# Two attention-fed mixes in one program: the first two sequence tiles joined in the second mix, softmax work moved, three weight sums put on TensorE

## The chip, the cores and the metric

One core of one Trainium2 chip. The metric is device time in microseconds of one execution, median over runs. TensorE (PE) multiplies, VectorE (DVE), ScalarE (ACT) and GpSimd (POOL) do the elementwise work, and SyncE (SP) issues every DMA.

## The reference

Three stages follow each other over 2 batches of 4160 tokens of width 192. The first is a causal seven-tap weighted sum whose weights are a softmax. The second ("first mix") mixes each token with its predecessor, multiplies by `w_k` (192 x 1024), squares the relu, multiplies by `w_v`, and gates with a sigmoid. The third ("second mix") multiplies by `w_in`, takes relu, convolves three taps over the tokens, gates, and multiplies by `w_out`.

```
w = softmax(weight_gen, axis=taps)                       # 8 heads x 7 taps
x = sum_k w[k] * x_padded[token + k]                     # (2, 4160, 192)
xk, xr = mu * x + (1 - mu) * x_prev                      # one pair of mu each
y = sigmoid(xr @ w_r) * (maximum(xk @ w_k, 0) ** 2 @ w_v)
h = maximum(y @ w_in, 0)
c = conv_w[0] * h[t-1] + conv_w[1] * h[t] + conv_w[2] * h[t+1]
out = (h * sigmoid(c)) @ w_out
```

The weights arrive as float64. A product keeps float32 accuracy by splitting each operand into a rounded part and its rest, so that each product is five matmul passes.

## The kernel before, in words

The sequence is cut into ten tiles (`SIZES`): 256, 248, seven of 472, and 352 tokens. All of the program is first written as a list of closures with due times (`at(t, fn)`, tile i around `T = 16*i`). `Program.schedule` then walks this list with its own table of costs (`cost`), and puts out the instructions in the order in which its clock would start them. Each engine gets its instructions in that fixed order: an instruction that waits holds up all that stand behind it on its engine. Every instruction is recorded by the one line in `schedule`, so views go by tile names, not lines.

- `softmax(j, ...)` works on block j of the weights `sw`: block 0 for tile 0, 1 for tile 1, 2 for tile 2, 3 for tiles 3 to 9. Its steps are a maximum (DVE), a subtraction (POOL; DVE for block 0), an Exp (ACT), a sum (DVE), a reciprocal (DVE) and a multiplication (POOL; DVE for block 0).
- `attention(i, b, ...)` makes tile i of batch b in "tokens" of 128 rows: four POOL operations each (`prod`, twice `prod<-prod`, `tok`). Tiles 0 and 1 have two such tokens in each batch, the 472-wide tiles four.
- `mixing(i, u, ...)` transposes `tok` on TensorE (`flip`: `pa<-ident,tok`), mixes neighbours, splits into rounded part and rest (the rest on POOL from tile 1 on: `xA<-mk,xA`, `mk<-mk,rm`). u=0 takes 128 columns of batch 0, u=1 of batch 1, u=2 the 64 left of each, so it needs all tokens of both. What u=2 makes goes by DMA to `xB`, without which no product of either batch is finished.
- `moe1(i, b, fi)` is one of eight blocks of the first mix: five passes into one of two banks `pa`, three ACT steps and one DVE step there (`s`), five passes into `am` and `ar`. `gate_r` makes the sigmoid gate, `mix_out` applies it and writes the tile into `x2[b]`.
- `moe2(i, b, fi)` is a block of the second mix: five passes into one of two banks `pc`, four ACT and four DVE steps (`h`, `pc`, `g`), five passes into `bm` and `br`. It runs `LAG` = 10 after `moe1`.
- `prepare` makes float32 weights of the float64 ones, 16 chunks: `narrow` builds the value of a chunk from its two halves with one ACT and five DVE operations, `split` writes rounded part and rest. The chunks of `w_k`, `w_v`, `w_r` come first, those of `w_in` and `w_out` after.

```
for i in range(NTILE):
    T = 16 * i
    ...
            for u, t in ((0, T - 5), (2, T - 3.7), (1, T + 3)) if i > 1 else ((0, 7), (2, 8.3), (1, 15)):
                mixing(i, u, t, 2.5)
    for b in range(NB):
        t = T + 8 * b
    ...
        for fi in range(NF):
            moe1(i, b, fi, t + fi)
            moe2(i, b, fi, t + fi + LAG)
        mix_out(i, b, t + 8.52)
        store(i, b, t + LAG + 10.02)
```

Of the kernel before, what the change touches and what calls it, by code (L numbers as in the profile page):

```python
# [26 lines left out]
LAG = 10  # L27
# [8 lines left out]
class Program:  # L36
# [37 lines left out]
    def cost(self, eng, method, out, ins, pointer):  # L74
# [12 lines left out]
        if eng == "DVE":  # L87
            if method == "tensor_reduce":
                n = self.count(ins[0])
# [6 lines left out]
        if eng == "POOL":  # L96
            busy = 0.1 + (n / 455 if method == "tensor_tensor" else n / 270)
            return busy, busy + 0.12
        return 0.6, 0.6

    def schedule(self):
# [4 lines left out]
        for i, (eng, method, a, k, _, hold) in enumerate(self.ops):  # L106
# [3 lines left out]
            ins = [x for x in aps if x is not out]  # L110
# [33 lines left out]
        for _ in range(n):  # L144
# [17 lines left out]
            for j in succ[i]:  # L162
                ready[j] = max(ready[j], t + dur[i] if eng == "PE" == self.ops[j][0] else end)
                left[j] -= 1
                if not left[j]:
                    open_[self.ops[j][0]].append(j)
# [17 lines left out]
def conv_moe_kernel(ctx: ExitStack, tc: tile.TileContext, xp, wg_first, wg_rest, mus, w_k, w_v, w_r, w_in, conv_w, w_out, out):  # L184
# [42 lines left out]
    ident = new("ident", [128, 128])  # L227
    wkA = new("wkA", [128, 2, DFF], F32R)
# [14 lines left out]
    wb_r = Ring([early[:, :1024].rearrange("p (a b) -> p a b", a=2)])  # L243
    rows_r = ring("rows", 2, [128, max(SLOTS) + PAD, DM])
# [9 lines left out]
    g_r = ring("g", 2, [128, 2, W], F32R)  # L254
# [54 lines left out]

    def narrow(st, n):  # L310
# [5 lines left out]
        ACT.activation(px, f(hi), ACTF.Copy, scale=2.0 ** -112)  # L316
        DVE.tensor_scalar(x, x, 3, None, op0=ALU.logical_shift_left)
# [57 lines left out]
    def prepare(first, seq):  # L375

        for j, (t, (load, n, go)) in enumerate(seq):
# [5 lines left out]
            def use(st=st, n=n, go=go):  # L383
                go(narrow(st[0], n))
# [10 lines left out]
    def softmax(j, a, b, eng, times, bank):  # L395
# [58 lines left out]
    def mixing(i, u, t, dt_):  # L454
        N, P, e = SIZES[i], PART[i], EXTRA[i]
        c = 1 if u == 2 else 0
        st = {}

        def flip():
            p = pa_r()  # L460
            st["p"] = p[:, e:e + N]
            st["q"] = p
            x = tok_t[i]
            k = (0, 256, 128)[u]
            for l in range(SLOTS[i]):
# [15 lines left out]
        def m1(k):  # L481
            st[k] = (am_r, ar_r)[k]() if i == 0 else mk_r()
            col = 2 * k + c
            own = slice(col, col + 1)
            if i < 2:
                a = shifted(lambda y, x: ACT.activation(y, x, ACTF.Copy, scale=onemu[:, own]))
                DVE.scalar_tensor_tensor(out=st[k][:, :N], in0=st["p"], scalar=mu[:, own], in1=a, op0=ALU.mult, op1=ALU.add)
            else:
                DVE.scalar_tensor_tensor(out=st[k][:, :N], in0=st["d"], scalar=onemu[:, own],
                                         in1=st["p"], op0=ALU.mult, op1=ALU.add)  # L490

        def hi(k):
# [6 lines left out]
            ACT.copy(x[:, 0, :N], st[k][:, :N])  # L499

        def lo(k):
            x = st["h", k]
            y = x[:, 1, :N] if u < 2 else (mk_r() if i == 0 else st[k])[:, :N].bitcast(F32R)
            (POOL if i else DVE).tensor_tensor(y, st[k][:, :N], f(x[:, 0, :N]), op=ALU.subtract)
            if u == 2:
                for b in range(NB):
# [5 lines left out]
                    SP.dma_start(out=f(z[oth, :N]), in_=f(y[own]))  # L512
# [98 lines left out]
    def mix_out(i, b, t):  # L611
        N = SIZES[i]
        X = x2[b]
        c = slice(2, N + 2)
# [11 lines left out]
        def a1():  # L626
            ACT.copy(X[:, 2, c], r[:, :N])
            ACT.copy(X[0:64, 3, c], r[0:64, :N])
# [18 lines left out]
    def moe2(i, b, fi, t):  # L647
        last = i == NTILE - 1
        N = SIZES[i] + (2 if last else 0)
# [201 lines left out]
```

## Time and profile before

| | |
|---|---|
| median of 3 runs | 779.31 us (778.96 to 781.27) |
| profiled execution | 780.29 us, of which its span 778.5 us |
| busy PE, ACT, DVE, POOL | 694.1, 665.5, 630.8, 506.6 us |
| mean granted clock of TensorE | 0.974 |
| idle time of PE by its largest releaser | 35.6 us, 4 times, POOL's `tok` |

All times in the profile count from the start of the span. Busy time is a sum over stages that differ much: the first 160 us, in which weights are prepared and two small tiles run, and the rest. So they are read by stretches and by single places in the program. In a row of a timeline, "x3" means three instructions merged, and the brackets at its end hold how long the engine was idle and what ended it.

### The profile page before, as it was taken

The page shows a single profiled execution, that of the slowest core. Times are in us where ns is not written, and L with a number is a line of the kernel's source. Part 1 is how long each engine was busy: PE and PEld are TensorE (multiplying, and loading weights), DVE is VectorE, ACT ScalarE, POOL GpSimd, SP SyncE. Part 2 cuts the span into 40 slices and gives each one's busy share as a digit, 9 for nine tenths or more (in the row PEclk, how much of TensorE's full clock was granted, in tenths as well). Part 3 has the DMA queues.
Part 4 walks back from the last instruction along what each step waited for, and adds up shares of the span by engine and source line. Part 5 has one row for each costly group of instructions (what it writes and reads, how often), then busy time and mean ns, then how long its engine had stood idle before and what let it go on. Part 6 is the DMA issues. An engine that isn't in the chain of part 4 may idle for free.

```text
span 778.5 us, 10782 instructions
## 1 busy us (share of the span) xinstructions
PE 694.1 (89%) x3505; PEld 606.3 (78%) x3505; DVE 630.8 (81%) x1137; ACT 665.5 (85%) x1441; POOL 506.6 (65%) x368
## 2 busy tenths in 40 slices
PE   0065776999999999999999999999999999999985
PEld 0054676898888888888888888888888888888974
DVE  6997977886878787878787888788788878788886
ACT  2466797998989898989998989898989899999985
POOL 6998888899999999999999798565702010110000
PEclk9996886999999999999999999999999999999999
DMA  7685010130130112111221120120002000200000
GB/s 224 197 269 180 4 52 11 58 105 11 62 101 18 53 70 51 70 51 52 69 70 51 39 78 20 45 63 7 20 0 70 1 19 1 57 0 19 19 2 28
DMA packets 19240, 45.09 MB, mean 58 GB/s; under 512 B 3056, under 2 KB 14704, under 8 KB 19056
## 3 DMA queue, kind: packets, MB, share of 16 engines
q1 hardware_dynamic: 19184, 44.41, 18.9%
q8 instruction: 27, 0.44, 0.2%
q14 instruction: 29, 0.24, 0.1%
HBM read 27.40 MB, written 6.39 MB: 43 GB/s over the span
## 4 chain that ended last, share of the span: by engine, by line
PE 68%; ACT 14%; DVE 14%; issue 2%; DMA 1%; SPq 0%; ACTq 0%; DVEq 0%
PE pa L169 21%; PE pc L169 16%; PE am L169 10%; PE bm L169 9%; PE ar L169 7%; PE br L169 6%; DVE pc L169 4%; ACT pa L169 2%; DVE stage L169 2%; ACT pc L169 2%; ACT h L169 2%; ACT g L169 2%; ACT L169 1%; DVE bm L169 1%; DVE s L169 1%
## 5 line engine op out<-in xcount | busy, mean ns | idle before, releaser
L169 DVE SCALAR_TENSOR_TENSOR pc<-h,cw,pc 128x472 f32<-128x472 f32 (+3 forms) x312 | 203.7, 653 | 34.9 <-ACT pc L169 31.9
L169 POOL TENSOR_TENSOR prod<-rows,sw 128x1344 f32<-128x1344 f32 x70 | 216.1, 3087 | 11.0 <-DMA rows<-in_x_dram 6.0
L169 ACT ACTIVATE pa<-pa 128x472 f32<-128x472 f32 (+3 forms) x324 | 162.7, 504 | 37.9 <-PE pa L169 33.8
L169 POOL TENSOR_TENSOR prod<-prod 128x576 f32<-128x576 f32 (+1 forms) x140 | 171.2, 1223 | 8.6
L169 PE MATMUL am<-s,wv 128*128 128x472 f32 (+3 forms) x480 | 146.9, 366 | 7.5 <-ACT s L169 6.0
L169 PE MATMUL bm<-g,wo 128*128 128x472 f32 (+3 forms) x465 | 144.5, 361 | 9.6 <-ACT g L169 9.0
L169 DVE TENSOR_TENSOR pc<-h,pc 128x472 f32<-128x472 f32 (+3 forms) x156 | 92.6, 594 | 54.4 <-ACT pc L169 53.0
L169 PE MATMUL pa<-xA,wkA 128*128 128x472 f32 (+3 forms) x480 | 124.4, 363 | 7.5 <-DVE s L169 3.5
L169 PE MATMUL pc<-x,wiA 128*128 128x474 f32 (+3 forms) x468 | 118.6, 361 | 3.2 <-DVE g L169 3.2
L169 POOL TENSOR_TENSOR xA<-mk,xA 128x472 fp32r<-128x472 f32 (+2 forms) x36 | 40.5, 1130 | 122.1 <-ACT xA L169 95.8
L169 PE MATMUL ar<-s,wv 128*128 128x472 f32 (+3 forms) x320 | 112.0, 362 | 5.0 <-DVE x L169 3.3
L169 PE MATMUL br<-g,wo 128*128 128x472 f32 (+3 forms) x310 | 109.4, 356 | 0.0
L169 DVE TENSOR_TENSOR s<-pa,s 128x472 fp32r<-128x472 f32 (+3 forms) x162 | 94.9, 586 | 16.0 <-ACT s L169 15.0
L169 PEld LDWEIGHTS am<-s,wv 128*128 128x128 f32 x480 | 88.7, 196 | 22.4 <-ACT s L169 11.2
L169 DVE TENSOR_TENSOR g<-pc,g 128x472 fp32r<-128x472 f32 (+3 forms) x153 | 90.4, 591 | 16.4 <-ACT g L169 14.9
L169 PEld LDWEIGHTS bm<-g,wo 128*128 128x128 f32 x465 | 86.5, 192 | 21.1 <-ACT g L169 11.5
L169 PEld LDWEIGHTS pa<-xA,wkA 128*128 128x128 f32 x480 | 86.4, 196 | 19.8 <-DVE s L169 6.3
L169 ACT ACTIVATE pc<-h,cw 128x472 f32<-128x472 f32 (+3 forms) x156 | 97.5, 625 | 1.6
L169 PEld LDWEIGHTS pc<-x,wiA 128*128 128x128 f32 x468 | 84.3, 194 | 14.0 <-DVE g L169 4.5
L169 ACT ACTIVATE h<-pc 128x474 f32<-128x474 f32 (+3 forms) x156 | 82.5, 529 | 9.6 <-PE pc L169 7.5
L169 PE MATMUL pa<-xB,wkB 128*128 128x472 f32 (+3 forms) x320 | 89.0, 359 | 1.1 <-DMA xB<-mk 1.1
L169 PE MATMUL pc<-x,wiB 128*128 128x474 f32 (+3 forms) x312 | 87.4, 359 | 0.0
(121 smaller groups left out, 1086.9 us busy)
## 6 DMA issues: line engine op xcount, KB each, us to landing
rows<-in_x_dram SPq DMA_DIRECT2D x14, 960.0 KB, 4.5
xB<-rm SPq DMA_DIRECT2D x28, 118.0 KB, 2.3
xB<-mk SPq DMA_DIRECT2D x28, 118.0 KB, 2.3
out_dram<-om SPq DMA_DIRECT2D x14, 236.0 KB, 2.0
rows<-in_x_dram SPq DMA_DIRECT2D x4, 768.0 KB, 6.6
rows<-in_x_dram SPq DMA_DIRECT2D x2, 864.0 KB, 4.3
out_dram<-ob SPq DMA_DIRECT2D x14, 118.0 KB, 2.2
stage<-in_moe_w_v_dram SPq DMA_DIRECT2D x4, 384.0 KB, 3.8
```

The source lines that it names most:

```text
L169: getattr(self.real[eng], method)(*a, **k)
```

## The change

- The second tile shrinks from 248 to 220 tokens, the seven wide ones grow from 472 to 476.
- In the second mix, tiles 0 and 1 become one unit of 476 (`UNIT`, `OFFSET`): tile 0 writes its part of `x2[b]`, and no `moe2` and no `store` run for it; `moe2` and `store` of tile 1 work on 476 tokens.
- `narrow` and `split` of the first three weight chunks (`on_pe`): the sum of the halves is a float32 matmul with the identity and one with the rounded identity, the rounded part is subtracted by a matmul with its negative, and ACT copies the rest out. Three DVE additions and four DVE subtractions go (two of the four are of one chunk). A tile `signs` holds the two matrices.
- The chunks of `w_in` and `w_out` are due later; blocks 1 and 3 of the softmax are due at other times; of block 3, tile 3 keeps its own Exp, and those of tiles 4 to 9 are done by one Exp over 46 columns of slots.
- The scheduler's costs of POOL, `tensor_reduce` and float32 matmuls change; a flip transposes its last token first; tile 0's mix keeps its values in one bank `ar`.
- Two more kinds of `mixing` (u = 3, 4) are written and not called.

```
-SIZES = [256, 248] + [472] * 7 + [352]
+SIZES = [256, 220] + [476] * 7 + [352]
+OFFSET = [0, SIZES[0]] + [0] * (NTILE - 2)
+UNIT = [None, SIZES[0] + SIZES[1]] + SIZES[2:]
...
+            if method == "matmul" and ins[0].dtype == F32:
+                n *= 4
...
-                n = self.count(ins[0])
+                return 0.05 + self.count(ins[0]) / 515, 0.15 + self.count(ins[0]) / 515
...
-            busy = 0.1 + (n / 455 if method == "tensor_tensor" else n / 270)
-            return busy, busy + 0.12
+            busy = 0.15 + (n / 455 if method == "tensor_tensor" else n / 270)
+            return busy, busy + 0.1
...
+        if on_pe[0]:
+            zr = wz_r()[:, :n]
+            DVE.tensor_scalar(x, x, 3, None, op0=ALU.logical_shift_left)
+            DVE.scalar_tensor_tensor(out=z, in0=hi, scalar=0x80000000, in1=x, op0=ALU.bitwise_and, op1=ALU.bitwise_or)
+            DVE.tensor_scalar(y, z, 0xFF800000, None, op0=ALU.bitwise_and)
+            DVE.scalar_tensor_tensor(out=zr, in0=lo, scalar=2.0 ** -52, in1=py, op0=ALU.mult, op1=ALU.mult)
+            PE.matmul(px, lhsT=ident, rhs=f(z), start=True, stop=False, skip_group_check=True)
+            PE.matmul(px, lhsT=signs[:, 0:128], rhs=zr, start=False, stop=True, skip_group_check=True)
+            return px
...
-        DVE.tensor_tensor(dst_lo, x, f(dst_hi), op=ALU.subtract)
+        if on_pe[0] and prog.space(x) == "PSUM":
+            PE.matmul(x, lhsT=signs[:, 128:256], rhs=dst_hi, start=False, stop=True, skip_group_check=True)
+            ACT.copy(dst_lo, x)
+        else:
+            DVE.tensor_tensor(dst_lo, x, f(dst_hi), op=ALU.subtract)
...
-        c = slice(2, N + 2)
+        c = slice(OFFSET[i] + 2, OFFSET[i] + N + 2)
...
-        N = SIZES[i] + (2 if last else 0)
+        N = UNIT[i] + (2 if last else 0)
...
-    softmax(1, 0, slots[1], POOL, (-82.6, -82.5, -82.4, -82.35, -82.3, -82.25), ar_r.tiles[0])
+    softmax(1, 0, slots[1], POOL, (-83.85, -83.65, -83.64, -83.63, -83.62, -83.55), am_r.tiles[0])
...
-        softmax(3, a, b, POOL, (16.5 + 0.3 * j, 16.6 + 0.3 * j, 19.5 + 0.1 * j, 20.5 + 0.5 * j, 20.6 + 0.5 * j, 24.9 + 16 * j), None)
+        softmax(3, a, b, POOL, (30.3, 30.4, 31.2, 32.0, 32.1, 34.9) if j == 0 else
+                (36.9 + 1.2 * j, 37 + 1.2 * j, None, 30 + 16 * j, 30.1 + 16 * j, 32.5 + 16 * j), None)
+    a = slots[3]
+    at(45.3, lambda: ACT.activation(sm[3][0][:, a:], sm[3][0][:, a:], ACTF.Exp))
...
-                moe2(i, b, fi, t + fi + LAG)
+                if i:
+                    moe2(i, b, fi, t + fi + LAG)
             mix_out(i, b, t + 8.52)
-            store(i, b, t + LAG + 10.02)
+            if i:
+                store(i, b, t + LAG + 10.02)
```

What the change does to the order shows at three places. The first is the beginning on DVE: block 0 of the softmax (`sw`, `am`, `smz`) ends with the multiplication of `sw` that the first token on POOL needs, and the first weight chunk begins with a shift in bank `bm`. Before:

```order
L169 TENSOR_REDUCE am<-sw 128x32
L169 TENSOR_SCALAR am<-am 128x32
L169 RECIPROCAL smz_108<-am 128x32
L169 TENSOR_TENSOR sw<-sw,smz_108 128x224
L169 TENSOR_SCALAR bm<-bm 128x512
```

And of the change:

```order
L175 TENSOR_REDUCE am<-sw 128x32
L175 TENSOR_SCALAR bm<-bm 128x512
L175 TENSOR_SCALAR am<-am 128x32
L175 SCALAR_TENSOR_TENSOR stage<-stage,bm 128x512
L175 RECIPROCAL smz_109<-am 128x32
L175 TENSOR_SCALAR pc_114<-stage 128x512
L175 TENSOR_TENSOR sw<-sw,smz_109 128x224
```

The shift (`bm<-bm`), which waits for a weight from memory, stood behind the multiplication of `sw`; now it and two more operations of the chunk stand ahead of it.

The second place is on POOL behind the fourth token of tile 2 before, and behind the eighth of it in the change; `sw<-sw,stage` are operations of block 3 of the softmax, `prod` and `tok` those of a token. Before:

```order
L169 TENSOR_TENSOR prod<-prod 128x384
L169 TENSOR_TENSOR sw<-sw,stage 128x448 x2
L169 TENSOR_TENSOR tok_79<-prod 128x192
L169 TENSOR_TENSOR sw<-sw,stage 128x448 x4
L169 TENSOR_TENSOR sw<-sw,stage 128x336
L169 TENSOR_TENSOR prod<-rows_76,sw 128x1344
L169 TENSOR_TENSOR sw<-sw,stage 128x448
```

And of the change:

```order
L175 TENSOR_TENSOR prod<-prod 128x576
L175 TENSOR_TENSOR prod<-prod 128x384
L175 TENSOR_TENSOR tok_82<-prod 128x192
L175 TENSOR_TENSOR xA_90<-mk_86,xA_90 128x476
L175 TENSOR_TENSOR xA_92<-mk_87,xA_92 128x476
L175 TENSOR_TENSOR sw<-sw,stage 128x448 x2
L175 TENSOR_TENSOR mk_86<-mk_86,rm_88 128x476
L175 TENSOR_TENSOR sw<-sw,stage 128x448 x2
L175 TENSOR_TENSOR mk_87<-mk_87,rm_89 128x476
L175 TENSOR_TENSOR sw<-sw,stage 128x448
```

Seven subtractions of block 3 stood among the tokens of tile 2, and so did seven multiplications further on; now none stands ahead of the last token of tile 2, and five subtractions follow it.

The third place is on PE around the flip for u=2 of tile 2, which needs the last token of batch 1 (`x_0` is `x2[0]`, and passes of 248 and 220 are those of tile 1). Before:

```order
L169 MATMUL am<-s_100,wv 128x248 x2
L169 MATMUL ar<-s_100,wv 128x248
L169 MATMUL am<-s_100,wv 128x248
L169 MATMUL ar<-s_100,wv 128x248
L169 MATMUL pa_111<-ident,tok_79 128x128 x4
L169 MATMUL bm<-g_101,wo 128x248 x2
L169 MATMUL pc_113<-x_0_73,wiA 128x250 x3
```

And of the change:

```order
L175 MATMUL bm<-g_78,wo 128x476 x2
L175 MATMUL br<-g_78,wo 128x476
L175 MATMUL pc_115<-x_0_74,wiA 128x478
L175 MATMUL pa_112<-ident,tok_82 128x128 x4
L175 MATMUL pc_115<-x_0_74,wiA 128x478 x2
L175 MATMUL pc_115<-x_0_74,wiB 128x478 x2
L175 MATMUL bm<-g_78,wo 128x476
L175 MATMUL br<-g_78,wo 128x476
```

The flip stood behind almost all of tile 1's first mix and all of tile 0's second mix; now it stands within the sixth block of the joined second mix. Counted over the whole order, 125,200 columns of matmuls stood ahead of it, and now 105,400 (without the 8,400 that the three chunks take, a float32 column counted four times).

## Rows read from the trace of the kernel before

**Rows 1.** Page: busy tenths of PE in 40 slices of 19.5 us.
```profile
PE   0065776999999999999999999999999999999985
```

**Rows 2.** Stretches: busy us of PE, PEld, DVE, ACT, POOL, then PEclk, DMA.
```profile
60.00:80.00 20.00, 12.17 (x56) 10.43 (x57) 16.10 (x41) 12.39 (x37) 17.89 (x17) 0.62 0.50 158
80.00:100.00 20.00, 14.98 (x95) 13.64 (x95) 18.42 (x38) 16.67 (x38) 17.10 (x14) 0.87 0.02 4
100.00:120.00 20.00, 13.24 (x88) 12.09 (x87) 15.81 (x36) 18.83 (x48) 16.90 (x15) 0.90 0.12 46
120.00:140.00 20.00, 15.91 (x86) 15.14 (x86) 12.98 (x30) 16.29 (x38) 18.18 (x15) 0.67 0.16 57
400.00:700.00 300.00, 298.21 (x1414) 258.28 (x1413) 243.77 (x398) 272.85 (x550) 139.40 (x99) 1.00 0.11 32
```

**Rows 3.** Timelines of three engines: start us, us, what, idle before.
```profile
9.45 0.63 ACT L169 ACTIVATE bm<-stage 128x512 f32<-128x512 f32 x1 [4.20 <-DMA stage<-in_moe_w_k_dram]
...
6.50 0.39 DVE L169 TENSOR_TENSOR sw<-sw,smz 128x224 f32<-128x224 f32 x1
10.11 0.70 DVE L169 TENSOR_SCALAR bm<-bm 128x512 uint32<-128x512 uint32 x1 [3.22 <-ACT bm L169]
...
7.34 3.02 POOL L169 TENSOR_TENSOR prod<-rows,sw 128x1344 f32<-128x1344 f32 x1 [5.96 <-DMA rows<-in_x_dram]
```

**Rows 4.** Timeline of POOL: products of two successive tokens; last token of tile 2.
```profile
37.27 3.02 POOL L169 TENSOR_TENSOR prod<-rows,sw 128x1344 f32<-128x1344 f32 x1
43.62 3.04 POOL L169 TENSOR_TENSOR prod<-rows,sw 128x1344 f32<-128x1344 f32 x1
...
139.14 0.59 POOL L169 TENSOR_TENSOR tok<-prod 128x192 f32<-128x192 f32 x1
```

**Rows 5.** Groups by shape, POOL: softmax factors applied to the fourth block.
```profile
L169 POOL TENSOR_TENSOR sw<-sw,stage 128x448 f32<-128x448 f32 x12 | 13.5, 1140 | 5.8 <-DVE stage L169 3.6 <-ACT h L169 2.2
```

**Rows 6.** Timeline of DVE: first rest of a product tile; first softmax maximum.
```profile
47.84 0.75 DVE L169 TENSOR_TENSOR s<-pa,s 128x256 fp32r<-128x256 f32 x2
...
85.90 1.01 DVE L169 TENSOR_REDUCE stage<-sw 128x64 f32<-128x448 f32 x1
```

**Rows 7.** Groups by shape, ACT and DVE: steps of both mixes; table loads.
```profile
L169 ACT ACT_TABLE_LOAD x14 | 18.0, 1283 | 3.8 <-DMA sw<-in_first_dram 3.6
L169 ACT ACTIVATE h<-pc 128x474 f32<-128x474 f32 x112 | 64.4, 575 | 5.5 <-PE pc L169 4.0
L169 ACT ACTIVATE h<-pc 128x258 f32<-128x258 f32 x16 | 6.2, 388 | 1.8 <-PE pc L169 1.6
L169 DVE SCALAR_TENSOR_TENSOR pc<-h,cw,pc 128x472 f32<-128x472 f32 x224 | 159.0, 710 | 28.1 <-ACT pc L169 25.9
L169 DVE SCALAR_TENSOR_TENSOR pc<-h,cw,pc 128x256 f32<-128x256 f32 x32 | 15.4, 480 | 2.4 <-ACT pc L169 2.3
L169 ACT ACTIVATE pa<-pa 128x248 f32<-128x248 f32 x32 | 11.7, 371 | 1.4 <-PE pa L169 1.1
```

**Rows 8.** Timeline of ACT: a table load and the Exp behind it.
```profile
96.85 1.28 ACT L169 ACT_TABLE_LOAD   x1
98.15 0.58 ACT L169 ACTIVATE sw<-sw 128x448 f32<-128x448 f32 x1
```

**Rows 9.** Timeline of PE: two places, a transpose of tile 2.
```profile
149.28 0.51 PE L169 MATMUL pc<-x,wiA 128*128 128x250 f32 x3
...
154.55 0.63 PE L169 MATMUL pa<-ident,tok 128*128 128x128 f32 x4 [1.17 <-DVE mk L169]
...
187.18 0.80 PE L169 MATMUL pa<-xA,wkA 128*128 128x472 f32 x3
```

**Rows 10.** ACT cast behind that transpose; DMA issues, KB, us to landing.
```profile
157.86 0.59 ACT L169 CAST rm<-mk 128x472 fp32r<-128x472 f32 x1 [0.34 <-DVE mk L169]
...
xB<-mk SPq DMA_DIRECT2D x28, 118.0 KB, 2.3
```

**Rows 11.** Timeline of PE: first pass that needs the mixed rest of tile 0.
```profile
44.70 1.19 PE L169 MATMUL pa<-xB,wkB 128*128 128x256 f32 x4 [1.07 <-DMA xB<-mk]
```

More of the change, by code (lines that the diff above doesn't have):

```diff
@@ L109, in schedule @@
             out = k["out"] if "out" in k else aps[0]
-            ins = [x for x in aps if x is not out]
+            ins = [x for x in [*a[0 if "out" in k else 1:], *(v for key, v in k.items() if key != "out")]
+                   if hasattr(x, "tensor") and hasattr(x, "ap")]
             dur[i], late[i] = self.cost(eng, method, out, ins, any(x is not None and x in ("scale",) and hasattr(k[x], "tensor") for x in k))
@@ L162, in schedule @@
             for j in succ[i]:
-                ready[j] = max(ready[j], t + dur[i] if eng == "PE" == self.ops[j][0] else end)
+                ready[j] = max(ready[j], t + dur[i] if eng in ("PE", "POOL") and eng == self.ops[j][0] else end)
                 left[j] -= 1
@@ L227, in conv_moe_kernel @@
     ident = new("ident", [128, 128])
+    signs = new("signs", [128, 256], F32R)
     wkA = new("wkA", [128, 2, DFF], F32R)
@@ L243, in conv_moe_kernel @@
     wb_r = Ring([early[:, :1024].rearrange("p (a b) -> p a b", a=2)])
+    g_r = ring("g", 2, [128, 2, W], F32R)
+    wz_r = Ring([t.rearrange("p a b -> p (a b)") for t in g_r.tiles])
     rows_r = ring("rows", 2, [128, max(SLOTS) + PAD, DM])
@@ L308, in fetch @@
         return st
+    on_pe = [False]
     def narrow(st, n):
@@ L381, in ld, with use @@
                 st[0] = load()
-            def use(st=st, n=n, go=go):
+            def use(st=st, n=n, go=go, j=j):
+                on_pe[0] = j < 3
                 go(narrow(st[0], n))
@@ L485, in m1 @@
             if i < 2:
-                a = shifted(lambda y, x: ACT.activation(y, x, ACTF.Copy, scale=onemu[:, own]))
-                DVE.scalar_tensor_tensor(out=st[k][:, :N], in0=st["p"], scalar=mu[:, own], in1=a, op0=ALU.mult, op1=ALU.add)
+                a = shifted(lambda y, x: ACT.activation(y, x, ACTF.Copy, scale=onemu[O, own]))
+                DVE.scalar_tensor_tensor(out=st[k][O, :N], in0=st["p"], scalar=mu[O, own], in1=a, op0=ALU.mult, op1=ALU.add)
             else:
-                DVE.scalar_tensor_tensor(out=st[k][:, :N], in0=st["d"], scalar=onemu[:, own],
+                DVE.scalar_tensor_tensor(out=st[k][O, :N], in0=st["d"], scalar=onemu[O, own],
                                          in1=st["p"], op0=ALU.mult, op1=ALU.add)
@@ L498, in hi @@
             st["h", k] = x
-            ACT.copy(x[:, 0, :N], st[k][:, :N])
+            ACT.copy(x[O, 0, :N], st[k][O, :N])
         def lo(k):
             x = st["h", k]
[L503 to L506, printed above, removed]
+            y = x[O, 1, :N] if u < 2 else (mk_r() if i == 0 else st[k])[O, :N].bitcast(F32R)
+            (POOL if i else DVE).tensor_tensor(y, st[k][O, :N], f(x[O, 0, :N]), op=ALU.subtract)
+            if u >= 2:
+                for b in range(NB) if u == 2 else (u - 3,):
                     z = xB_r[k]()
@@ L626, in a1 @@
         def a1():
+            ACT.copy(X[0:64, 3, c], r[0:64, :N])
             ACT.copy(X[:, 2, c], r[:, :N])
-            ACT.copy(X[0:64, 3, c], r[0:64, :N])
         def d2():
```

59 lines of the change are left out of this document (33 added, 26 removed).

## The prediction

> **What bounds the kernel now.** I read the slices of the page first, then stretches, then timelines of single places. The slices show a head of some 150 us in which PE is partly idle, after which it stays at nine tenths or more until the end [rows 1]. From 400 to 700 us PE is busy for 298.21 of 300 us with 1414 matmuls, 0.212 us each [rows 2]. A tile of 472 has 352 of them, twelve of 128 columns and the others of 472 or 474, so the mean is 460 columns and the pace about 2,170 columns per us. The total of columns hardly changes (1.43 million by the two orders), nor does the tail. So the change is worth what the head becomes shorter by, and this can be read as a lead: the time at which the same count of columns stands behind PE, before and after.
>
> In the head no engine is the bound throughout. From 100 to 120 us ACT is busy for 18.83 of 20 us, from 80 to 100 us DVE for 18.42, and PE for 13 to 15 [rows 2]. The granted clock averages 0.62 from 60 to 80 us and 0.67 from 120 to 140 us [rows 2], a mixture of the full level, 2.4 GHz, and half of it. Sharp places in the work of before are a second-mix block of tile 1 at 149.28 us, with 117,200 columns ahead of it by the order, and a first-mix block of tile 2 at 187.18 us, with 190,600 ahead [rows 9].
>
> **The change, part by part.**
>
> *The start.* POOL's first token began at 7.34 us, behind a multiplication of `sw` at 6.50 us [rows 3]. In the new order this multiplication stands behind the shift of the first weight chunk, which could start only at 10.11 us, since the weight came from memory at 9.45 us [rows 3]. Ahead of the multiplication are three operations of 512 columns at 0.70 us and two small ones, then itself at 0.39 us: 10.11 + 2.1 + 0.3 + 0.4 = 12.9 us. The first token is 5.6 us late. A token takes 43.62 - 37.27 = 6.35 us [rows 4]. Between tile 0's four tokens there is now one softmax operation, half as wide as the 1.14 us of [rows 5] and so some 0.7 us, against several and some waits before: 12.9 + 25.4 + 0.7 = 39.0 us, against 37.27 us, so 1.7 us late. The first pass that needs `xB`, at 44.70 us [rows 11], comes at about 46.
>
> *TensorE's sums.* They take seven DVE operations of 0.3 to 0.7 us away, about 4 us, and add four copies to ACT. No row shows a float32 matmul of 512 columns. Below, it costs what a rounded one does, 0.24 us by the pace above; above, four times that at half the clock, 1.9 us. PE waits for POOL's tokens there, so it is hidden; only the next use of the bank waits for it. I take 1 us for each, which leaves DVE ready with the first chunks at about 38 us, before POOL's last token at 39. So this part is worth nothing at the end; without POOL's cover it would be worth up to 4 us.
>
> *The first mix of tile 0.* From its first `s` to the first maximum of softmax block 3, DVE took from 47.84 to 85.90 us [rows 6], 38.1 us. Between the same marks stand 74 rows of DVE in the old order and 76 in the new, of like widths: the weight chunks of the second mix are still there, tile 0's second mix is gone, more of the first is in. I take 38 us from 49 us, so 87 us.
>
> *The first mix of tile 1, batch 0.* Ten blocks follow with few weights among them. A block is five passes (0.6 us), three ACT steps of 0.37 us [rows 7], and one DVE step of 0.4 us, with hand-overs 2.5 us, in two banks, so 1.3 us each. With the seven maxima, 15 us: the joined second mix begins at 102 us. 70,700 columns stand ahead of it.
>
> *POOL up to tile 2.* The 14 operations of softmax block 3 at 1.14 us [rows 5] stood among tile 2's tokens, the last of which ended at 139.73 us [rows 4]. Now: 39.0 + 0.7 + 2 x 1.14 (blocks 1 and 2) + 4 x 6.35 for tile 1 = 67.4; and 8 x 6.4 + 6 x 0.7 (rests of tile 1, by their width against the 1.14 us) for tile 2 = 122.8 us, 17 us earlier.
>
> *The wait that replaces the old ones.* PE would reach the flip for u=2 of tile 2 (34,700 columns after 102 us, at 1.9 per ns) at 120 us. It must wait for POOL until 123 us, and tile 2's `xB` comes a chain later. Before, the chain from flip to the end of the cast was 157.86 + 0.59 - 154.55 = 3.9 us [rows 9, 10]; with a rest on POOL, DMA issue and 2.3 us of landing [rows 10] it is 8 us. So the pass on `xB`, with 118,300 columns ahead of it, runs at 131 us. Before, that count stood at 149.28 + 0.5 = 149.8 us [rows 9]. **The lead is 18.5 us.**
>
> *From there to PE's steady pace.* A wide block replaces two narrow ones: ACT's `h` costs 575 ns in place of two of 388, a DVE tap 710 in place of two of 480 [rows 7]. That relieves ACT and DVE where they were the bound. ACT's table loads, 14 at 1283 ns [rows 7], become 6 by the order, since six of the seven Exps are one: 10.3 us off ACT. Its operation after a load starts 1.30 us behind it [rows 8]. The Trainium skill, *ScalarE: Activation LUTs*, *What ACT_TABLE_LOAD costs*, adds a drain of about 1.38 us to each switch, which would make this 21 us; this trace shows no such drain. In the new order 191,200 columns stand ahead of tile 2's batch 1; from 131 us at 2.0 per ns that is 168 us. Before, the same count is at 187.5 us [rows 9]. The lead is 19.5 us.
>
> *What is given back.* The joined Exp is 2576 columns wide, about 2.2 us by the slope of `h` (187 ns for 216 columns, rows 7), and has two table loads around it: 4.8 us of ACT in the steady part, where ACT is busy for 272.85 of 300 us [rows 2]. PE has a few banks of work in hand; I take 3 us, between 0 and 4.8. Tile 3's last token ends at 122.8 + 5 x 1.14 + 4 x 1.2 (rests of tile 2) + 8 x 6.4 + 3.5 (two rests and a multiplication) = 188 us, and PE wants it at about 187; I take 1.5 us, between 0 and 5. Sum: 19.5 - 3 - 1.5 = **15 us**.
>
> The profiled execution took 780.29 us, 1.0 more than the median; 15 us off gives 765.3 for it and **764 us** for the median.
>
> **Rivals.**
>
> *More (750 to 757 us).* The chain behind the flip is hidden by work that stands between flip and pass (12,900 columns, 6 us), the joined Exp falls into slack, and the wide pace holds: 19.5 + 5 = 24 us. For it: ACT and DVE are far less loaded than before in 100 to 160 us. Against it: PE's order is fixed, and the flip itself waits. By the drain of the page on ScalarE another 11 us of ACT (an estimate, 8 x 1.38) would go, and the time would be about 753 us; the 1.30 us of the trace speak against it.
>
> *Less (770 to 776 us).* PE is thinly used while only the first mix runs. Before, its clock fell to half in such stretches [rows 2]. At tile 0's pace of about 2.4 us for all 27 blocks the second mix begins at 115 us, `xB` is passed at 139 us, and the lead of 10.8 us leaves about 7: 772 us. The Trainium skill, *TensorE: Matmul & The Clock Gate*, *HAM oscillation*, describes this return to the low clock after waits, and the trace agrees (0.62 from 60 to 80 us).
>
> *Slower (782 to 788 us).* With tile 0's second mix gone, PE has nothing but the first mix until tile 1's batch 0 is through `mix_out`. Break-even is where the gain of the later stretch no longer makes up for this: 191,200 columns at 187.5 - 4.5 = 183 us, so the joined mix from 124 us. That is 2.8 us for each of the 27 blocks from 49 us; at 3.0 us the end is 5 us late, 784 us. Before, 15 blocks took 38 us, 2.5 each, with second-mix work among them, so this would need a worse stall than any now seen.
>
> *No change.* The 5.6 us of the start and the waits on POOL eat up all that ACT and DVE gain, because POOL's tokens set the pace throughout. Against it: POOL loses 16 us of softmax ahead of tile 2.
>
> **How the numbers follow.** The forecast (758 to 769 us) has 0.60, *more* 0.14, *less* 0.14, *no change* 0.05, *slower* 0.07. A measurement tells 0.3%, 2.3 us, from no change. Faster is 0.60 + 0.14 + 0.14 = 0.88, same 0.05, slower 0.07. The range from 753 to 773 us leaves out the last two, a part of *more* and a part of *less*, together about 0.2.
>
> **What would show it.** POOL's first token at about 13 us; tile 0's last at 38; `h` of the joined mix first at 102 us; PE idle for `tok` at about 120 us, and passing tile 2's `xB` at 131; six table loads; PE at nine tenths from 135 us on, but for a gap at the joined Exp. The prediction is wrong if the joined mix begins after 115 us, or if POOL's tokens are late for tile 3 by more than 5 us.

## The result, and the profile after

The changed kernel takes 767.34 us (median of 4 runs, 766.81 to 769.35) against 779.33 (4 runs): a ratio of 0.985 [0.982, 0.987], 12.0 us faster where 15 were forecast. The profiled execution took 766.81 us with a span of 765.0. Run again later, it had 767.12 (766.91 to 767.37, ratio 0.983 [0.982, 0.985]).

The page after: PE's busy tenths in 40 slices, and the shares of the chain of work that ended last:

```profile
PE   4177888998899999999999899999999999999996
...
POOL 43%; PE 40%; ACT 7%; issue 5%; DVE 2%; DMA 2%; SPq 0%; ACTq 0%; POOLq 0%
```

Nines begin in the eighth slice, as in [rows 1], but the seven slices of the head (134 us; a slice is 19.1 us wide) are fuller than there. New dips stand in the tenth and eleventh slices, and one in the 23rd. In the chain, followed back from the last instruction, POOL has 43%; on the page before it was not among the listed engines, and PE had 68%, ACT and DVE 14% each: the last work now hangs on POOL's tokens (its `prod` alone has 34%). The stretches of the changed kernel (PE, PEld, DVE, ACT, POOL, then PEclk) show where PE was busy:

```profile
60.00:80.00 20.00, 14.56 (x94) 12.67 (x93) 15.28 (x34) 14.87 (x45) 19.26 (x18) 0.91 0.66 199
80.00:100.00 20.00, 16.09 (x117) 13.89 (x115) 15.95 (x34) 13.75 (x45) 19.22 (x14) 1.00 0.14 51
100.00:120.00 20.00, 17.50 (x108) 14.95 (x108) 14.93 (x28) 16.53 (x41) 19.06 (x14) 1.00 0.13 50
120.00:140.00 20.00, 18.28 (x91) 14.36 (x90) 17.79 (x31) 19.57 (x42) 18.57 (x14) 1.00 0.22 50
...
180.00:200.00 20.00, 16.18 (x74) 12.72 (x73) 15.36 (x25) 18.50 (x31) 15.93 (x12) 1.00 0.37 103
200.00:240.00 40.00, 36.90 (x166) 29.63 (x165) 37.97 (x62) 33.37 (x65) 38.28 (x27) 1.00 0.14 42
```

From 60 to 140 us PE was busy for 56.3 us at granted clocks of 0.62 to 0.90 [rows 2], and now for 66.4 us at 0.91 to 1.00. Behind that, PE now idles where it did not before: 6.9 us from 180 to 240 us (before 0.7) and 4.6 us from 300 to 450 us (before 0.8).

The places of the prediction, from the timelines of POOL, PE and ACT:

```profile
10.98 3.04 POOL L175 TENSOR_TENSOR prod<-rows,sw 128x1344 f32<-128x1344 f32 x1 [9.63 <-DVE sw L175]
118.89 0.59 POOL L175 TENSOR_TENSOR tok<-prod 128x192 f32<-128x192 f32 x1
...
36.79 1.11 PE L175 MATMUL pa<-ident,tok 128*128 128x128 f32 x4 [12.45 <-POOL tok L175]
43.66 1.15 PE L175 MATMUL pa<-xB,wkB 128*128 128x256 f32 x4
120.58 0.60 PE L175 MATMUL pa<-ident,tok 128*128 128x128 f32 x4
128.65 0.61 PE L175 MATMUL pa<-xB,wkB 128*128 128x476 f32 x2
163.31 0.81 PE L175 MATMUL pa<-xA,wkA 128*128 128x476 f32 x3
...
102.67 0.57 ACT L175 ACTIVATE h<-pc 128x478 f32<-128x478 f32 x1 [0.33 <-PE pc L175]
```

| place | forecast | measured | before |
|---|---|---|---|
| POOL's first token | 12.9 | 10.98 | 7.34 [rows 3] |
| tile 0's pass on xB | 46 | 43.66 | 44.70 [rows 11] |
| first `h` of the joined mix | 102 | 102.67 | none |
| POOL's last token of tile 2 | 122.8 | 119.48 | 139.73 [rows 4] |
| POOL's last token of tile 3 | 188 | 185.71 | 200.61 |
| tile 2's pass on xB | 131 | 128.65 | 149.8, same count of columns |
| tile 2's batch 1 begins | 168 | 163.31 | 187.5, same count of columns |

The lead at tile 2's pass was 21 us, not 18.5. PE had no wait for the flip: the last token ended at 119.48 us, PE came to it at 120.58, and from there to the pass it idled for 1.3 us in all. Where tile 2's batch 1 begins the lead was 24.2 us, not 19.5. Four later waits of PE, and two groups on ACT:

```profile
185.77 0.66 PE L175 MATMUL pa<-ident,tok 128*128 128x128 f32 x4 [1.97 <-POOL tok L175]
195.52 0.92 PE L175 MATMUL pa<-xA,wrA 128*128 128x476 f32 x3 [1.81 <-ACT r L175]
351.53 0.92 PE L175 MATMUL pa<-xA,wrA 128*128 128x476 f32 x3 [1.39 <-DVE mk L175]
429.99 0.92 PE L175 MATMUL pa<-xA,wrA 128*128 128x476 f32 x3 [2.62 <-DVE mk L175]
...
L175 ACT ACT_TABLE_LOAD x6 | 7.7, 1283 | 0.8 <-PEq L882 0.7
L175 ACT ACTIVATE sw<-sw 128x2576 f32<-128x2576 f32 x1 | 2.4, 2357 | 0.0
```

They have different releasers: tile 3's last token (POOL), the sigmoid behind the joined Exp (ACT), and twice a mixed value `mk` (DVE). The same waits stand in the later series of this kernel (run 12), the second of them with 0.66 us instead of 1.81. The lead shrinks from 24.2 us to 13.5 in the spans.

### The profile page after: what moved, and what is told of

Same layout as the page of the kernel before. It is cut to its first block, busy times and chain, and to the rows that moved or that the text cites. A ratio compares the mean times of both kernels' runs of the same rounds, so it can differ in the third digit from the quotient of the medians.

```text
span 765.0 us, 10294 instructions
## 1 busy us (share of the span) xinstructions
PE 697.2 (91%) x3358; PEld 590.4 (77%) x3358; DVE 621.6 (81%) x1066; ACT 650.8 (85%) x1364; POOL 506.6 (66%) x362
## 4 chain that ended last, share of the span: by engine, by line
POOL 43%; PE 40%; ACT 7%; issue 5%; DVE 2%; DMA 2%; SPq 0%; ACTq 0%; POOLq 0%
POOL prod L175 34%; PE pa L175 13%; PE pc L175 9%; PE bm L175 6%; PE am L175 6%; POOL tok L175 4%; PE br L175 4%; PE ar L175 3%; POOL xA L175 2%; POOL sw L175 1%; ACT pa L175 1%; POOL mk L175 1%; ACT pc L175 1%; ACT s L175 1%; DMA stage<-in_moe_w_k_dram 1%
## 5 line engine op out<-in xcount | busy, mean ns | idle before, releaser
L175 POOL TENSOR_TENSOR prod<-rows,sw 128x1344 f32<-128x1344 f32 x70 | 216.3, 3090 | 14.6 <-DVE sw L175 9.6
L175 DVE SCALAR_TENSOR_TENSOR pc<-h,cw,pc 128x476 f32<-128x476 f32 (+1 forms) x280 | 196.7, 703 | 30.2 <-ACT pc L175 27.5
L175 ACT ACTIVATE pa<-pa 128x476 f32<-128x476 f32 (+3 forms) x324 | 162.6, 504 | 40.9 <-PE pa L175 37.0
L175 PE MATMUL am<-s,wv 128*128 128x476 f32 (+3 forms) x480 | 148.0, 366 | 9.3 <-ACT s L175 8.5
L175 PE MATMUL bm<-g,wo 128*128 128x476 f32 (+1 forms) x417 | 138.3, 379 | 6.4 <-ACT g L175 6.0
L175 PE MATMUL pa<-xA,wkA 128*128 128x476 f32 (+3 forms) x480 | 121.8, 361 | 8.3 <-DVE s L175 4.2
L175 PE MATMUL pc<-x,wiA 128*128 128x478 f32 (+1 forms) x420 | 116.1, 377 | 1.4 <-DVE g L175 1.2
L175 PE MATMUL ar<-s,wv 128*128 128x476 f32 (+3 forms) x320 | 110.8, 356 | 0.1
L175 DVE TENSOR_TENSOR s<-pa,s 128x476 fp32r<-128x476 f32 (+3 forms) x162 | 94.7, 586 | 19.6 <-ACT s L175 17.5
L175 PE MATMUL br<-g,wo 128*128 128x476 f32 (+1 forms) x278 | 104.5, 376 | 0.0
L175 ACT ACTIVATE pc<-h,cw 128x476 f32<-128x476 f32 (+1 forms) x140 | 92.4, 660 | 1.5
```

The lines of the kernel that those rows point to most:

```text
L175: getattr(self.real[eng], method)(*a, **k)
```

## The experiments

Where nothing else is said, a kernel starts from the changed one (767.2 us over both of its series). Each was timed beside the kernel before on one chip, which gives its ratio; the interval of one ratio is 1.2 to 1.9 us wide to each side, so a difference between two kernels of less than about 2 us can't be told from none. In the profiled executions with the same beginning ACT took up the first weight 7.5 to 9.1 us after the start; a token that is up to 1.5 us later in a run can come from that alone.

**1. The three chunks on VectorE.**

```
-                on_pe[0] = j < 3
+                on_pe[0] = False
```

> The changed kernel (767.3 us), but the first three weight chunks are summed and split on VectorE as before. Theory of the prediction (POOL's tokens cover these chunks, the sums are worth nothing at the end): 767 us, at most 1.5 us from the changed kernel; tile 0's first pass on its mixed rest is within 1.5 us of 43.7 us. Rival (the chunks are on the path, the sums gave about 4 us of the 12): 770 to 772 us, and that pass is 3 to 4 us later.

770.88 us, ratio 0.988 [0.986, 0.990]: 3.7 us slower than the changed kernel, as the rival said; its sign, a pass 3 to 4 us later, did not come. PE of this kernel:

```profile
36.87 1.12 PE L175 MATMUL pa<-ident,tok 128*128 128x128 f32 x4 [12.46 <-POOL tok L175]
45.14 1.05 PE L175 MATMUL pa<-xB,wkB 128*128 128x256 f32 x4
```

POOL's tokens come at the same time (36.87 against 36.79), and yet the pass on xB is 1.5 us later, and the first `h` of the joined mix at 105.73, 3.1 us later. Between flip and pass stand VectorE's mix steps. One operation of a chunk, 0.4 us, now stands among them; the rest is a small addition of the softmax, in the changed kernel and in this one:

```profile
41.25 0.24 DVE L175 TENSOR_SCALAR smz<-smz 128x64 f32<-128x64 f32 x1
41.67 1.38 DVE L175 TENSOR_SCALAR smz<-smz 128x64 f32<-128x64 f32 x1
```

It takes 1.1 us more, since it now stands beside an operation of POOL that ends at 42.99 us (the last section has more of this kind). The delay does not simply stay: at 67 us it is 0.4 us (1.1 against run 12), and it grows to 3.1 us by 105 us, in a stretch where the granted clock was 0.90 and 0.76 (85 to 95 us) instead of 1.00. Why it grows there is not shown.

**2. Softmax and weight chunks due as before.**

```
...
-                                     (16.0, chunk_out(w_out, wo, 2)), (18.0, chunk_out(w_out, wo, 3))])
...
+                                     (9.0, chunk_out(w_out, wo, 2)), (10.0, chunk_out(w_out, wo, 3))])
...
-    softmax_load(3, wg_rest[:, (slots[1] + slots[2]) * KH:], 18.2, 50.0)
+    softmax_load(3, wg_rest[:, (slots[1] + slots[2]) * KH:], 10.2, 40.0)
...
-        softmax(3, a, b, POOL, (30.3, 30.4, 31.2, 32.0, 32.1, 34.9) if j == 0 else
...
+        softmax(3, a, b, POOL, (16.5 + 0.3 * j, 16.6 + 0.3 * j, 19.5 + 0.1 * j, 20.5 + 0.5 * j, 20.6 + 0.5 * j, 24.9 + 16 * j), None)
```

> The changed kernel, but block 3 of the softmax and the weight chunks of the second mix have the due times of before, with one Exp for each tile, so that 14 POOL operations of 1.14 us stand ahead of tile 2's last token again and 14 table loads run. Theory (POOL's load ahead of tile 2 makes the lead): tile 2's last token 14 to 16 us later (about 134 us), the lead of 21 us falls to about 6, the give-back of 180 to 240 us is gone too, and the end is at 773 to 778 us. Rival (the joined second mix makes the lead): within 3 us of 767 us, or faster, since the waits of 180 to 240 us go.

773.72 us, ratio 0.991 [0.989, 0.993], within what the theory gave; tile 2's last token at 130.48 us, 11 later, and PE is busy for 59.75 of 60 us from 180 to 240, so the give-back is gone, with PE itself late (tile 2's xB is passed at 145.59 us, tile 3's flip comes 4.4 us behind its token). But the first `h` of the joined mix came only at 120.00 us, which neither theory said. In its head the clock was low:

```profile
60.00:80.00 20.00, 10.88 (x53) 9.33 (x54) 15.50 (x35) 12.13 (x37) 17.98 (x15) 0.74 0.52 147
80.00:100.00 20.00, 16.54 (x91) 14.75 (x92) 18.54 (x37) 15.56 (x45) 18.87 (x17) 0.76 0.01 2
100.00:120.00 20.00, 16.79 (x92) 15.12 (x92) 14.82 (x25) 9.29 (x27) 19.06 (x13) 0.73 0.13 50
```

**3. Chunks early alone.** The chunks' part of that edit (all eight due times of before), without the softmax.

> The changed kernel, but the weight chunks of the second mix have the due times of before (4.4 to 10 instead of 6 to 18); the softmax stays as changed. Theory (the chunks' 12 us on VectorE between 60 and 100 us only change places with blocks of the first mix, and all have to be done before the joined second mix): second mix begins within 2 us of 102.7 us, the end within 1.5 us of 767.3. Rival (early chunks hold back the first mix; that, and not the softmax, is what cost the kernel with both early its 5 us): second mix begins 5 us or more later, the end at 770 to 773.

772.08 us, ratio 0.989 [0.988, 0.991]: 4.9 us slower, first `h` at 107.12. The rival's time holds and its 5 us nearly (4.5), its reason does not: VectorE starts the chunks at the same times (shifts of `bm` and `br` at 62.70, 72.20, 74.69 and 81.13 us against 62.75, 72.44, 73.71 and 80.56), since a due time only ranks what is ready. Only the order around them differs, and with it the clock. Two stretches of this kernel, then of the changed one:

```profile
85.00:90.00 5.00, 4.07 (x18) 3.60 (x18) 4.34 (x11) 3.24 (x12) 4.76 (x5) 0.50 0.00 0
90.00:95.00 5.00, 5.00 (x26) 4.89 (x26) 4.09 (x7) 1.87 (x6) 4.76 (x4) 0.55 0.44 158
```

```profile
85.00:90.00 5.00, 4.48 (x31) 3.78 (x32) 4.94 (x10) 3.77 (x14) 4.76 (x4) 1.00 0.00 0
90.00:95.00 5.00, 4.86 (x37) 4.33 (x38) 4.62 (x8) 2.68 (x9) 4.69 (x5) 1.00 0.52 197
```

PE is as busy from 85 to 95 us, but does 44 matmuls where the changed kernel does 68. PE waited for 1.32 and 0.64 us ahead of it (before 82.05 and 84.40) and for 0.93 us within it (before 89.12); the changed kernel had waits of 1.09, 0.18 and 0.80 us (before 81.85, 82.65 and 85.06) and kept its clock. So the low clock is measured, and what brought it about is not. Beside this kernel, moving the softmax back costs (run 2) only 1.6 us more.

**4. Tiles 0 and 1 not joined.** Tile 0 has `moe2` and `store` of its own; the chunks are early, since its second mix needs them.

```
-OFFSET = [0, SIZES[0]] + [0] * (NTILE - 2)
-UNIT = [None, SIZES[0] + SIZES[1]] + SIZES[2:]
+OFFSET = [0] * NTILE
+UNIT = SIZES
...
```

> The changed kernel, but tiles 0 and 1 (256 and 220) have second mixes of their own again, with the weight chunks of the second mix due as before; the softmax is as in the changed kernel. Theory (joining relieves ACT and DVE by 16 blocks of four ACT and four DVE steps at about 0.2 us each, some 13 us of each engine between 60 and 160 us, of which a part is on the path): 770 to 775 us, with more ACT and DVE time from 80 to 140 us than in the changed kernel. Rival (POOL alone sets the head, and second-mix work fills PE earlier): 764 to 768 us.

773.74 us, ratio 0.992 [0.991, 0.994]: within the theory's range, but beside run 3, which shares its chunks, joining is worth 1.7 us, which can't be told from none, and not 6. From 60 to 140 us ACT and VectorE were busy for 64.80 and 67.42 us against 64.72 and 63.95 in the changed kernel, but the two kernels do different work in that stretch. Over the whole span ACT was busy for 657.6 us and VectorE for 627.1, in run 3 for 650.8 and 623.0: joining spares 6.8 and 4.1 us, not 13 of each.

**5. The factor first.**

```
-            at(t, use)
+            at(t, use, 9.0 if j == 0 else 0.0)
```

> The changed kernel, but the order puts block 0's multiplication of sw ahead of the first weight chunk's shift. The first token of POOL starts about 1.5 us earlier (9.4 us instead of 10.98). Theory (POOL's chain of tokens reaches from the start to tile 3): all of its tokens to 120 us are 1 to 1.5 us earlier and the end is 1 us earlier, 766 us. Rival (other engines set the pace from tile 0 on): same time, 767.3 us within 0.5 us.

768.91 us, ratio 0.986 [0.984, 0.987]: no gain. POOL's first token began at 9.31, 1.7 us earlier, and PE's pass on tile 0's xB at 42.07, but the flip for u=0 of tile 2 was at 104.31 against 103.24. The lead at the start was lost before 105 us, in a stretch with clocks of 0.79, 0.83 and 0.91 (40 to 100 us). The rival is nearer; the 1.7 us above the changed kernel can't be told from none.

**6. Two factors early.** One Exp for tiles 3 and 4 ahead of tile 2's last tokens; five subtractions among tile 4's tokens.

```
...
+    a = slots[3] + slots[4]
+    at(22.35, lambda: ACT.activation(sm[3][0][:, :a], sm[3][0][:, :a], ACTF.Exp))
+    at(55.5, lambda: ACT.activation(sm[3][0][:, a:], sm[3][0][:, a:], ACTF.Exp))
```

> The changed kernel, but the factors of tiles 3 and 4 are made by one early Exp, their subtractions ahead of tile 2's last three tokens, and the five other subtractions stand among tile 4's tokens, with the joined Exp (of five tiles) behind them. Theory (the gap of PE from 180 to 200 us, 3.8 us, comes from POOL, which had only the softmax of block 3 to do for 5 us between tile 2's last token and tile 3's first): tile 2's last token 1 to 2 us later (121), tile 3's first product at 125 us instead of 130.89, its last token at 181 instead of 185.7, PE idle for less than 2 us in 180 to 200 us, and the end 1 to 3 us earlier than the changed kernel's 767.3. Rival (the wait only passes on to the Exp and to VectorE's backlog): within 1 us of 767.3.

768.66 us, ratio 0.986 [0.984, 0.987]. The gap of 180 to 240 us closed (PE 59.73 of 60 us), but not as the theory said: tile 3's last token ended at 187.78 us, not 181, some 2 us later than in the changed kernel, and PE came to its flip only at 192.48 us, 6.7 us later. Two other gaps opened (timelines of POOL and PE, then three stretches of this kernel):

```profile
187.19 0.59 POOL L175 TENSOR_TENSOR tok<-prod 128x192 f32<-128x192 f32 x1
192.48 0.60 PE L175 MATMUL pa<-ident,tok 128*128 128x128 f32 x4
...
100.00:160.00 60.00, 51.82 (x268) 43.49 (x268) 44.88 (x80) 49.45 (x107) 52.88 (x37) 0.94 0.17 48
180.00:240.00 60.00, 59.73 (x282) 51.12 (x281) 48.63 (x79) 55.68 (x109) 58.35 (x43) 1.00 0.21 62
240.00:280.00 40.00, 35.23 (x159) 27.75 (x158) 38.67 (x58) 35.14 (x68) 38.43 (x26) 1.00 0.17 56
```

In the changed kernel PE's were 55.78, 53.08 and 39.75. So PE found the token ready because it had itself become late from 100 to 160 us; what held it up there is not shown. VectorE's backlog moved with the Exp, to 240 to 280 us, where it is busy for 38.67 of 40. The wait passed on, as the rival had it.

**7. The sums spread.** Sum, addition and reciprocal of tiles 5 to 9, and the multiplication behind them, are held back in the order.

```
...
+                at(t, fn, hold if t > times[1] + 5 else 0.0)
...
+                (0.0, 0.0, 215.0, 268.0, 322.0, 375.0, 410.0)[j])
```

> The changed kernel, but the sums, additions and reciprocals of tiles 5 to 9 in block 3, which VectorE does one after the other from 197 to 238 us, are held in the order until shortly before their factors are used, some 55 us apart. Theory (VectorE, busy 37.97 of 40 us there, makes PE idle for 3.1 us from 200 to 240): VectorE at 34 to 35 of 40 us there, PE idle under 1 us, the end 1.5 to 3 us earlier than 767.3. Rival (the backlog is elsewhere, PE waits there for what came late from the joined Exp): PE idle still about 3 us and the end within 1 us of 767.3.

764.83 us, ratio 0.981 [0.979, 0.982]: 2.4 us faster than the changed kernel, with each of its four executions below each of that kernel's eight; the best of all runs. The theory holds (two stretches of this kernel):

```profile
180.00:200.00 20.00, 17.48 (x74) 13.93 (x73) 13.78 (x24) 18.40 (x32) 15.87 (x12) 0.91 0.33 93
200.00:240.00 40.00, 40.00 (x187) 34.09 (x186) 34.30 (x56) 37.48 (x75) 38.27 (x28) 1.00 0.16 47
```

VectorE went from 37.97 to 34.30 us and PE's 3.1 us of idle time from 200 to 240 us are gone.

**8. The edits of runs 5 to 7 together** (the spread for tiles 6 to 9).

> The changed kernel with three edits: block 0's factor ahead of the first weight chunk, the factors of tiles 3 and 4 early, and the sums of tiles 6 to 9 spread. Theory (each of the two later gaps is its own): PE idle in 180 to 240 us falls from 6.9 us to 3 or less, the end at 762 to 764 us. Rival (after tile 2 the pace of PE with its few banks gives back whatever is gained): 766 to 768 us.

770.95 us, ratio 0.987 [0.984, 0.989]: slower than the changed kernel. PE idles for 0.3 us from 180 to 240 us, as the theory wanted, but again because it comes late (to tile 3's flip at 194.82 us, the token having ended at 189.48): from 100 to 160 us it is busy for only 50.70 us at a clock of 0.89. The gains do not add up. Of six runs two, with mean granted clocks of 0.992 and 0.993, took 766.8 and 767.2 us, and four, with 0.962 to 0.986, took 770.9 to 771.8; the profile is of one of these four.

**9. Filler matmuls.** The kernel of run 2, with, behind each block of tiles 0 and 1 but the last of its eight:

```
...
+            if i < 2 and fi < NF - 1:
+                for _ in range(5):
+                    PE.matmul(acc["m"][:, :N], lhsT=zeros, rhs=xin[i, b, 0, 0][:, 0, :N], start=False, stop=False)
```

> The kernel with softmax and weight chunks early (773.7 us), and five more matmuls with a weight of zeros behind each of 28 blocks of the first mix of tiles 0 and 1, which add zero to am: 35,000 columns more, some 16 us of TensorE at the full clock. Theory (the half clock in that stretch, 0.73 to 0.76 granted from 60 to 120 us, is what made its joined second mix begin 17 us late): the granted clock from 60 to 120 us rises to 0.95 or more, the second mix begins 5 to 15 us earlier in spite of the work added, and the end is 3 to 6 us earlier, 768 to 771 us. Rival (the clock is low because TensorE waits, and costs nothing): the end within 1 us of 773.7 or up to 8 us later, by the columns added.

775.58 us, ratio 0.995 [0.993, 0.997], 1.9 us slower than without. In the profiled execution (779.31 us, the slowest of eight) the clock rose only to 0.78, 0.88 and 0.91 in the three stretches, and the joined mix began at 122.10 us. No gain was seen; since some 15 us of work were added as well, this does not tell what a clock alone would give.

**10. The Exp later.** From run 7.

```
-    at(45.3, lambda: ACT.activation(sm[3][0][:, a:], sm[3][0][:, a:], ACTF.Exp))
+    at(45.3, lambda: ACT.activation(sm[3][0][:, a:], sm[3][0][:, a:], ACTF.Exp), 190.0)
```

> The kernel with spread sums (764.8 us), but the joined Exp stands on ScalarE behind the casts rm and the two rests of tile 3, some 8 us later in the order. Theory (on ScalarE it holds up tile 3's mixed rest and the sigmoid r, which is 1.5 to 1.8 of the 2.5 to 3.8 us that PE is idle from 180 to 200 us; tile 4's tokens, which get 4 to 5 us later by it, still have room): PE idle there falls to about 2.1 us (what is left is the wait for tile 3's last token), the end 1 to 2 us earlier, 763 to 764. Rival (tile 4's tokens have no room, since POOL is busy for 38.3 of 40 us there): a wait for tok or xB of 3 us or more appears between 220 and 270 us, and the end is at 765 to 768.

769.97 us, ratio 0.987 [0.985, 0.988]: 5.1 us slower than run 7, and by neither mechanism: no wait for tok or xB came up; the Exp stands in front of a sigmoid instead of a cast. ACT and PE of this kernel:

```profile
199.45 1.28 ACT L175 ACT_TABLE_LOAD   x1
200.74 2.35 ACT L175 ACTIVATE sw<-sw 128x2576 f32<-128x2576 f32 x1
203.11 1.28 ACT L175 ACT_TABLE_LOAD   x1
204.40 0.55 ACT L175 ACTIVATE pc<-pc 128x476 f32<-128x476 f32 x1
204.87 0.56 ACT L175 ACTIVATE r<-pa 128x476 f32<-128x476 f32 x1
...
205.48 1.56 PE L175 MATMUL pa<-xA,wkA 128*128 128x476 f32 x3 [3.55 <-ACT r L175]
```

The block of 4.9 us on ACT costs PE 3.55 us here, against 1.81 and 0.66 in the two executions of the changed kernel. Beside run 7, PE idles for 2.9 us more from 180 to 240 us (busy 54.54 against 57.48), and from 200 to 240 us its clock was 0.91 instead of 1.00.

**11. Three buffers mk.** From run 10.

```
-    mk_r = ring("mk", 2, [128, NMAX])
+    mk_r = ring("mk", 3, [128, NMAX])
```

> The same with three buffers mk instead of two. Theory (PE's waits for VectorE's mk at 350 and 430 us, 4.0 us together in the changed kernel, come from VectorE waiting until POOL has read the buffer for its rest, since only two buffers exist): these waits are gone or below 1 us, PE at 49.5 of 50 us or more throughout 350 to 450 us, the end 2 to 4 us earlier than without the third buffer, 760 to 762. Rival (the mixed rest itself is late from POOL, the buffer is not it): the waits stay, or turn into waits for xA or xB, and the end is the same within 1 us.

765.35 us, ratio 0.981 [0.980, 0.983]: 4.6 us faster than run 10. From 350 to 450 us PE was busy for 97.84 us instead of 95.61, two thirds of the way to the 99 of the theory. From 200 to 240 us it was as busy (36.46 and 36.45), but at a clock of 0.96 instead of 0.91. So some 2 us came with the buffer, but not by the theory: in run 10 `mk` held PE for only 0.97 us there (before 434.97), here for 0.78; what went is a wait of 2.42 us for VectorE's `g` (before 356.52 in run 10). The rest is not settled.

**12. The changed kernel again**, beside runs 3, 10 and 11.

> The changed kernel itself, on the same chip as these three, as their common measure: 766.5 to 768.5 us.

767.12 us, as given above.

## Why the prediction was right, and where it was not

**Right.** The kernel is faster because PE does more in the head, and up to tile 2's pass on xB the places lie within 3.4 us of the forecast: POOL's last token for tile 2 came 20 us earlier than before, the joined mix began at 102.67 us, tile 2's xB was passed 2 us before the forecast. Slower, by a joined mix withheld until 124 us, did not come; run 2, whose joined mix began at 120 us, shows how near an unlucky order comes to it. No change did not come either.

**Luck in the sum.** I had 19.5 us of lead and 4.5 given back. Measured were 24.2 us, at tile 2's batch 1, and 10.7 given back. Two errors of about 5 and 6 us nearly cancel; that the sum came near is luck in that part. (The lead of 18.5 us in the prediction should read 149.8 - 131 = 18.8, and tile 0's last token stands there as 39.0 and as 38; nothing hangs on either. It came at 36.73.)

**The step that failed: TensorE's sums, "worth nothing at the end".** They are worth 3.7 us (run 1), close to the "up to 4 us" that I gave for the case without cover. I had let VectorE be ready before POOL's last token. But it is not a chunk that has to be ready then; it is VectorE itself, whose mix steps stand in one queue with chunk work and softmax. By run 1, 1.5 us are lost between flip and pass, most of it by one small addition that falls beside an operation of POOL. How the delay comes to 3.1 us at the joined mix, and what part chunk work and the clock have in it, stays open.

**A second step that failed: the wait that was to replace the old ones.** "It must wait for POOL until 123 us" did not come: POOL was 3.3 us earlier than forecast, PE came to the flip 1.1 us behind the token, and other work filled all but 1.3 us of the 8.1 us from flip to pass. That is the first condition of *more*, and a lead of 24 us, as it had it, was there at 163.31 us. *More* failed behind that, by what was given back.

**What the other parts gave.** By what undoing them costs: sums 3.7, later chunks 4.9 (with an order in which the clock stayed high), joining about 1.7, the softmax moved about 1.6; together 11.9. That this is near 12.0 shows nothing: the last two are no larger than what a comparison can tell, the parts need not add up (run 8), and the tile sizes, the scheduler's costs and the order of the transposes were never undone by themselves. My sum had set the lead down to POOL's softmax above all. That part did give tile 2 its lead, but POOL is busy nearly all the time until 450 us, so that what it is spared ahead of tile 2 it has to do ahead of tiles 3 and 4: 20.3 us of lead at tile 2's last token, 14.9 at tile 3's.

**The size that was off: the give-back.** I took 4.5 us: 3 for the joined Exp and 1.5 for tile 3's tokens. The two waits exist and are 1.8 (0.7 in run 12) and 2.0 us. Two more were not in the sum: the sums behind the joined Exp, which VectorE does in one run up to 238 us (3.1 us of PE; run 7 takes them away), and `mk` at 350 and 430 us (4.0 us). From tile 2's batch 1 to the end, PE idles for 20.9 us (before 14.6) and is busy for 580.8 us (before 576.4): of the 10.7 us given back, 6.3 are idle time. The other 4.4 us, of a busier PE, are not explained.

**The price of a float32 matmul.** I bounded it by 0.24 and 1.9 us and took 1. The first one is recorded as two instructions, 2.05 us together, and the rounded one behind it starts 1.74 us after it:

```profile
9.90 2.05 PE L175 MATMUL bm<-stage,ident 128*128 128x512 f32 x2 [9.90 <-DVE stage L175]
11.64 0.77 PE L175 MATMUL bm<-g,signs 128*128 128x512 f32 x1
```

This was hidden: PE waits for POOL until 36.8 us. The start on POOL was 1.9 us earlier than forecast since the first weight landed earlier: ACT took it up at 7.68 us instead of 9.45 [rows 3]. That differs between executions: with the same beginning it was 9.06 us in run 10 and 9.14 in run 2.

**Table loads.** There are six, as forecast. The operation behind one starts 1.29 us after it (199.45 and 200.74 in run 10). The Trainium skill, *ScalarE: Activation LUTs*, *What ACT_TABLE_LOAD costs*, gives a drain on top; by that, the kernel would have gained more, and neither the time nor a trace shows it.

**The clock.** Before, it was low in the head, now hardly; how much of the gain that is, stays open. Run 3 suggests several us, and so do the two groups of run 8, but neither separates the clock from the waits that go with it; in run 7 single executions with mean clocks of 0.972 and 0.995 took 764.6 and 764.5 us.

## What to carry to other kernels

A stage may be called hidden only if none of its operations stand in a queue ahead of the work that ends the wait; ask what is queued on the engine, not whether its result is ready. Check a sum at the places between: here lead and give-back were off by about 5 and 6 us, and the total by 3. A gap that is gone need not be mended: in runs 6 and 8 PE no longer waited because it had become late itself. Work that is put off from a crowded stretch comes back as a block: give it a place for each part, as run 7 did, and look at what stands behind it. With orders fixed by a scheduler's clock, small edits change the order elsewhere and their gains do not add up, so time the combination.

## What the runs showed of the hardware

**VectorE waits for GpSimd.** Small additions on 64 columns of SBUF took up to 2.24 us in the changed kernel (mean 1039 ns of six, before 546, shortest 0.19). The long ones end with an operation on POOL. Timelines of DVE and POOL:

```profile
197.54 1.88 DVE L175 TENSOR_SCALAR stage<-stage 128x64 f32<-128x64 f32 x1
204.69 2.24 DVE L175 TENSOR_SCALAR stage<-stage 128x64 f32<-128x64 f32 x1
...
196.27 3.10 POOL L175 TENSOR_TENSOR prod<-rows,sw 128x1344 f32<-128x1344 f32 x1
203.80 3.08 POOL L175 TENSOR_TENSOR prod<-rows,sw 128x1344 f32<-128x1344 f32 x1
```

199.42 and 206.93 are the ends on DVE, 199.37 and 206.88 those on POOL. The Trainium skill, *GPSIMD Engine Reference*, *Specifications*, names this: the SBUF interfaces are shared with VectorE, with contention for its instructions in a two-port mode or with two SBUF inputs. The trace agrees: such an instruction can take ten times its own time where POOL never rests.

**A wait of a few us can cost more than itself.** After the 3.55 us of run 10 the three passes at 205.48 took 1.56 us, and the granted clock was 0.50 from 205 to 210 us, the lower of its two levels; such a group takes 0.81 us at full (163.31 in the changed kernel). After the 2.62 us at 429.99 us, the granted clock of the changed kernel was 0.66 from 430 to 435 us. The Trainium skill, *TensorE: Matmul & The Clock Gate*, *HAM oscillation*, describes such a fall after a wait for data; here the waits are for other engines. Not every one does it: after the 2.42 us before 356.52 in run 10 the granted clock stayed at 1.00.
